# A 64-point second stage on paired column tiles, an inverse on paired row tiles, and PSUM banks given out singly or in pairs, in a kernel of infini-attention and a long convolution

## The chip, the cores and the metric

One core of one Trainium2 chip. The time is the device time of one execution in microseconds (us), from the first to the last instruction of the core. The kernel before takes 365.05 us (median of 3 runs, 364.62 to 369.96).

A run is called slow when it is over 1.5% above the fastest of the same kernel. Below, "ratio" is the mean time of one kernel's fast runs over that of the other's fast runs of the same rounds, so it is not quite the ratio of the medians that I quote. A bracket behind it is its 95% interval. Medians are over all runs, slow ones too.

## The reference, cut to what matters

Two independent parts share the kernel, and their results are laid side by side.

```python
def _A_ref(x, wq, wk, wv, wo, beta):      # 2048 x 576, 32 heads of 18, 4 segments of 512
    q, k, v = ...                         # x @ wq, x @ wk, x @ wv, split into heads and segments
    for s in range(4):
        p = softmax(qs @ ks.T * scale + mask)
        a_dot = p @ vs                    # attention in the segment
        a_mem = (phi(qs) @ M) / (phi(qs) @ z + 1e-6)   # memory of earlier segments
        outs.append(g * a_mem + (1 - g) * a_dot)
        M, z = M + phi(ks).T @ vs, z + sum(phi(ks))
    return o @ wo

def _B_ref(q, k, v, shift_k, ssm_k, ssm_D):   # 2048 x 576
    kv = (causal filter of 4 taps over k) * v
    y = irfft(rfft(kv, 4096) * rfft(ssm_k, 4096))[:2048]   # a long convolution per channel
    return q * (y + kv * ssm_D)
```

## The kernel before

A list scheduler inside the program decides, while the kernel is built, in which order each engine gets its operations. It works with estimated durations and with two long tables of offsets (`SHIFT`, `BIAS`) that were tuned for this kernel. What reaches the chip is a fixed order per engine, and in the traces of this case an engine, or a queue that issues DMAs, that waits for one operation doesn't go on to the next (VectorE below stands 14.4 us although a later operation could run). This will matter.

The Fourier transform is done by matmuls in two stages of the forward transform (`f1`, `f2`) and an inverse. The second stage works on the whole array, with two accumulated matmuls for each result:

```python
def f2(self, A_h, A, k1):
    ...
    for o, tabs in ((0, (self.CS, self.SN)), (1, (self.NSN, self.CS))):
        for n, tab in enumerate(tabs):
            nc.tensor.matmul(pp[:, x, GB * o:GB * o + GB], lhsT=tab[:, k1, :], rhs=src[:, 16 * n + k1, :],
                             start=(n == 0), stop=(n == 1))
    ...   # one PSUM bank and one copy of 384 columns for each of kernel spectrum and input spectrum
```

The 576 columns of x are four tiles of 128 and a remainder of 64. The first 512 rows of x are transposed on TensorE. For the three later segments a transposing DMA brings x in transposed. For the remainder it takes the last 128 columns (448 to 575), of which 64 were in tile 3 already, and the weights of those 64 are zero, so that every matmul of the projections uses the whole array:

```python
def first_x(self, ident):
    x = Tl(self.pl.big, [P, 4, D], BF16, "x0")     # a slot of the ring that holds the sine tables too
    ...
def load_x(self, s):
    for t in range(5):
        c0 = 128 * t if t < 4 else 448
        self.dma(128, lambda dq, t=t, c0=c0: dq.dma_start_transpose(
            out=xT[:, t, :], in_=self.A_x[0, L * s:L * s + L, c0:c0 + P]), w=[(xT, t)], transpose=True)
def proj_qk(self, s, m):
    ...  [nc.tensor.matmul(pq[:], lhsT=self.wqk[:, t, 128 * m:128 * m + P], rhs=xT[:, t, :],
                           start=(t == 0), stop=(t == 4)) for t in range(5)]
```

The softmax here doesn't subtract the row's maximum and nothing guards it: scores larger than these inputs give would overflow.

Of the kernel before, what the change touches and what calls it, by code (L numbers as in the profile page):

```python
# [39 lines left out]
class Slots:  # L40


    def __init__(self, pool, tag, bufs, fifo=True):
        self.pool, self.tag, self.fifo = pool, tag, fifo
        self.slots = [None] * bufs
        self.made, self.given = 0, 0


class Tl:
    def __init__(self, ring, shape, dtype, name):  # L50
        self.ring, self.shape, self.dtype, self.name = ring, shape, dtype, name
        self.left, self.end, self.tile = 0, 0.0, None
        self.no = ring.made
        ring.made += 1
# [4 lines left out]
    def slot(self):  # L59

        r = self.ring
        if r.fifo and r.given != self.no:
            return None
        best = None
        for i, o in enumerate(r.slots):
            if o is None:
                return i, 0.0
            if o.left == 0 and (best is None or o.end < best[1]):
                best = i, o.end
        return best  # L70

    def give(self, i):
        r = self.ring
        r.given += 1
        r.slots[i] = self
        self.tile = r.pool.tile(self.shape, self.dtype, tag="%s%d" % (r.tag, i), name=self.name)
# [6 lines left out]
class Graph:  # L83
# [33 lines left out]
    def run(self):  # L117
# [5 lines left out]
        while left:  # L123
            best = {}
            for o in cand:
                t0, sl = 0.0, []
                for t in o.tiles:
                    if t.tile is None:
                        s = t.slot()
# [14 lines left out]
            for eng, lst in best.items():  # L144
                m = min(x[0] for x in lst)
                lst = [x for x in lst if x[0] <= m + 0.3]
                x = min(lst, key=lambda x: (x[1].prio, x[0]))
                if pick is None or x[0] + x[2] * 0.0 < pick[0][0]:
                    pick = x, eng
            (st, o, us, emit, sl), eng = pick  # L150
            if len(o.alts) > 1:

                h = self.bias.get(o.label, self.bias.get(None, 0.0))
                c = [(x[0] + x[2] + (h if e == ACTQ else 0.0), x, e) for e, l in best.items() for x in l if x[1] is o]
                _, (st, o, us, emit, sl), eng = min(c, key=lambda z: z[0])
# [20 lines left out]
NK1 = 16  # L176
QS = GB // 4
CT0 = [0, 128, 256, 384, 448]
F1D, HXD, NPS, NPJ = 1, 0, 2, 4
# [14 lines left out]
class Pools:  # L194
    def __init__(self, ctx, tc):
# [5 lines left out]
        self.pss = Slots(self.ps, "s", NPS, fifo=False)  # L201
        self.psj = Slots(self.ps, "j", NPJ, fifo=False)
        ring = lambda tag, n: Slots(self.sb, tag, n)
        self.x = ring("x", 1)
        self.stage = ring("st", 5)
# [11 lines left out]
        self.ct = ring("ct", 2)  # L217
        self.HX = ring("H", 3)
        self.Y = ring("Y", 3)
# [3 lines left out]
class Part:  # L223
# [3 lines left out]
    def psj(self, shape, name, dtype=F32):  # L227
        return Tl(self.pl.psj, shape, dtype, name)
# [28 lines left out]
class PartA(Part):  # L257
    def __init__(self, tc, pl, G, ident, A_x, A_wq, A_wk, A_wv, A_wo, A_beta, out):
# [23 lines left out]
        zero(("wz", 0), self.wqk[0:64, 4, :], 2 * D)  # L282
        zero(("wz", 1), self.wv[0:64, 4, :], D)
# [10 lines left out]
        def load_w(dst, w, c0, c1, key, also=()):  # L294
# [3 lines left out]
                dq.dma_start(out=dst[64:128, 4, :], in_=w[512:576, c0:c1])), w=[key], n=2, also=also)  # L298
# [70 lines left out]
    def first_x(self, ident):  # L369

        nc = self.nc
        x = Tl(self.pl.big, [P, 4, D], BF16, "x0")
        self.dma(576, lambda dq: dq.dma_start(out=x[:], in_=self.A_x[0, 0:L, :].rearrange("(t p) c -> p t c", p=P)), w=[x])
        xT = self.xs[0] = Tl(self.pl.x, [P, 5, L], BF16, "xT")
        self.G.label = "tr0"
        for t0, n in ((0, 2), (2, 2), (4, 1)):
            pt = self.psj([P, 2, 4, P], "pt", BF16)

            def tr(t0=t0, n=n, pt=pt):
                for t in range(t0, t0 + n):  # L380
                    c0 = 128 * t if t < 4 else 448
                    for k in range(4):
                        nc.tensor.transpose(out=pt[:, t - t0, k, :], in_=x[:, k, c0:c0 + P], identity=ident[:])
# [5 lines left out]
    def load_x(self, s):  # L389
# [3 lines left out]
        for t in range(5):  # L393
            c0 = 128 * t if t < 4 else 448
            self.dma(128, lambda dq, t=t, c0=c0: dq.dma_start_transpose(
                out=xT[:, t, :], in_=self.A_x[0, L * s:L * s + L, c0:c0 + P]), w=[(xT, t)], transpose=True)


    def store_rows(self, s, kind, tile, r0, f0, n, key):

        qd = self.qk_dram[s]
        self.dma(n, lambda dq: dq.dma_start(out=qd[D * kind + f0:D * kind + f0 + n, :], in_=tile[r0:r0 + n, :]),
# [770 lines left out]
```

## Time and profile before

| | before |
|---|---|
| median of 3 runs | 365.05 us |
| span of the profiled run, mean granted clock | 360.9 us, 0.923 |
| TensorE busy | 296.2 us, 82% |
| VectorE busy | 274.0 us, 76% |
| ScalarE busy | 233.9 us, 65% |
| GpSimd busy | 227.2 us, 63% |

Read it like this: no engine is full over the whole span, yet TensorE is nearly full between 30 and 317 us (the prediction shows the stretches), so a change has to shorten TensorE's work, or fill the ends, to gain. The first is the page's account of the DMA queues (second line: packets, MB, share of 16 engines over the span):

```profile
DMA packets 99860, 56.61 MB, mean 157 GB/s; under 512 B 72286, under 2 KB 92702, under 8 KB 99806
q1 hardware_dynamic: 95518, 54.65, 58.4%
```

```profile
L395 SPq DMA_TRANSPOSE xT<-in_A_x_dram x15: 1142/1259/2603, 49.7 to 176.8; - x15
```

Fifteen loads (5 tiles in 3 segments), all of the kind DMA_TRANSPOSE. The queue SPq, on which SyncE issues them, is held for 1.3 us by each.

### The profile page before, as it was taken

What the parts mean: (1) busy time and instruction counts of PE and PEld (TensorE: products, weight loads), DVE (VectorE), ACT (ScalarE), POOL (GpSimd) and SP (SyncE); (2) the same over time, 40 slices, a digit from 0 to 9 for tenths busy, and PEclk for the clock granted to TensorE, in tenths of its full rate; (3) what the DMA queues carried; (4) which work ended last, traced back from release to release, by engine and by line L of the source; (5) the groups of instructions that cost most, each with busy time, mean ns of one, the idle gap of its engine ahead of it and who ended that gap; (6) DMA issues with size and microseconds to landing.
All of it is one profiled execution on the core that took longest, in us unless ns stands there. A gap on an engine that the chain in (4) does not pass through costs nothing.

```text
span 360.9 us, 7982 instructions
## 1 busy us (share of the span) xinstructions
PE 296.2 (82%) x3048; PEld 171.8 (48%) x3072; DVE 274.0 (76%) x486; ACT 233.9 (65%) x296; POOL 227.2 (63%) x294
## 2 busy tenths in 40 slices
PE   0239998979988987999999697899998979975494
PEld 0136453554444553456644343365565635564283
DVE  7538763866899984778977868559799779789574
ACT  0626048778977877687978846678998767842030
POOL 3500013317999999574396845539799987999800
PEclk9999998999999999899999978599999965999569
DMA  8589656996677419363897764494362543216415
GB/s 241 141 161 172 192 138 146 229 235 201 117 152 205 121 37 202 122 200 96 156 236 202 190 188 161 154 281 171 88 174 59 167 140 123 102 36 202 147 45 144
DMA packets 99860, 56.61 MB, mean 157 GB/s; under 512 B 72286, under 2 KB 92702, under 8 KB 99806
## 3 DMA queue, kind: packets, MB, share of 16 engines
q1 hardware_dynamic: 95518, 54.65, 58.4%
q10 hardware_dynamic: 4304, 1.45, 1.6%
q8 instruction: 24, 0.39, 0.5%
q14 instruction: 14, 0.11, 0.1%
HBM read 25.96 MB, written 21.80 MB: 132 GB/s over the span
## 4 chain that ended last, share of the span: by engine, by line
PE 47%; DMA 17%; DVE 17%; issue 5%; SPq 3%; POOL 3%; ACTq 3%; ACT 3%; DVEq 0%; POOLq 0%
PE sc L518 9%; DMA rt<-a_r_scratch 7%; PE pq L411 6%; PE pout L667 5%; PE pp L910 5%; PE po L568 5%; DMA a_r_scratch<-cs 4%; PE pc L869 4%; PE pf L895 3%; PE pv L450 3%; PE pi L934 3%; ACTq L297 2%; DVE HX L245 2%; POOL Y L947 2%; DMA Dt<-in_B_ssm_D_dram 2%
## 5 line engine op out<-in xcount | busy, mean ns | idle before, releaser
L521 ACT ACTIVATE PT<-sc 128x1024 bf16<-128x1024 f32 x160 | 157.9, 1029 | 33.0 <-PE sc L518 21.5
L526 POOL TENSOR_SCALAR_AFFINE_SELECT PT<-PT 128x512 bf16<-128x512 bf16 (+1 forms) x112 | 80.8, 738 | 68.3 <-ACT PT L521 67.1
L947 POOL TENSOR_TENSOR Y<-HX 128x768 bf16<-128x768 bf16 x48 | 81.9, 1712 | 14.2 <-PE pi L934 9.4
L518 PE MATMUL sc<-qk 18*128 18x512 bf16 (+3 forms) x512 | 60.6, 316 | 5.8 <-ACT PT L521 5.2
L411 PE MATMUL pq<-xT,wqk 128*128 128x512 bf16 x162 | 43.7, 386 | 4.5 <-DVE V L245 2.1
L245 DVE CAST HX<-pp 128x384 bf16<-128x384 f32 x75 | 38.9, 548 | 7.0 <-PE pp L910 6.3
L518 PEld LDWEIGHTS <-qk 18*128 18x128 bf16 x512 | 16.7, 93 | 42.1 <-issue 41.0
L934 PE MATMUL pi<-Y,CST 128*128 128x192 bf16 x96 | 25.0, 266 | 11.2 <-POOL Y L953 8.2
L954 POOL TENSOR_TENSOR Y<-Y 128x192 bf16<-128x192 bf16 x48 | 29.6, 617 | 0.0
L953 POOL TENSOR_TENSOR Y<-Y 128x192 bf16<-128x192 bf16 x48 | 28.4, 592 | 1.4
L245 DVE CAST q<-pq 128x512 bf16<-128x512 f32 x27 | 18.5, 687 | 13.7 <-PE pq L411 12.7
L895 PE MATMUL pf<-W1bd,xs 128*128 128x256 bf16 x144 | 21.8, 288 | 8.0 <-DVE xs L993 7.2
L910 PE MATMUL pp<-A_h,CS 128*128 128x192 bf16 x96 | 24.3, 258 | 3.2 <-DVE A_kv L245 1.4
L411 PEld LDWEIGHTS <-wqk 128*128 128x128 bf16 x180 | 16.5, 99 | 21.9 <-issue 7.7
L450 PE MATMUL pv<-wv,xT 128*128 128x288 bf16 x160 | 26.8, 316 | 0.0
L568 PE MATMUL po<-PT,V 128*32 128x256 bf16 (+3 forms) x512 | 26.0, 328 | 0.4 <-DVE kv L872 0.2
L910 PE MATMUL pp<-A_kv,CS 128*128 128x192 bf16 x96 | 23.6, 253 | 2.7 <-DVE V L245 1.4
L667 PE MATMUL pout<-wo_sb,od 126*128 126x288 bf16 (+1 forms) x160 | 23.6, 291 | 0.2 <-issue 0.2
L910 PEld LDWEIGHTS <-CS 128*128 128x128 bf16 x192 | 18.9, 101 | 9.8 <-issue 9.0
L655 DVE TENSOR_TENSOR nt<-nt,rt 126x1024 bf16<-126x1024 bf16 (+1 forms) x15 | 13.6, 904 | 10.3 <-DMA rt<-a_r_scratch 10.3
L245 DVE CAST A_kv<-pi 128x384 bf16<-128x384 f32 x33 | 17.9, 550 | 3.8 <-PE pi L934 3.3
L450 PEld LDWEIGHTS <-xT 128*128 128x128 bf16 x160 | 16.3, 106 | 9.1 <-issue 2.9
(141 smaller groups left out, 550.6 us busy)
## 6 DMA issues: line engine op xcount, KB each, us to landing
a_o_scratch<-ou SPq DMA_DIRECT2D x12, 512.0 KB
qk<-a_qk_scratch SPq DMA_DIRECT2D x48, 108.0 KB
a_qk_scratch<-q SPq DMA_DIRECT2D x32, 128.0 KB
nt<-a_o_scratch SPq DMA_DIRECT2D x12, 252.0 KB
rt<-a_r_scratch SPq DMA_DIRECT2D x12, 252.0 KB
xs<-kv_scratch SPq DMA_DIRECT2D x3, 768.0 KB
q_sb<-in_B_q_dram SPq DMA_DIRECT2D x3, 768.0 KB
out_dram<-oA SPq DMA_DIRECT2D x16, 144.0 KB
```

Source lines behind the costliest of these rows:

```text
L245: return self.G.op([(DVEQ, dve_us(n, 0.53 if bf else 1.042), lambda: nc.vector.tensor_copy(out=out(), in_=in_())), (ACTQ, act_us(n), lambd ...
L411: nc.tensor.matmul(pq[:], lhsT=self.wqk[:, t, 128 * m:128 * m + P], rhs=xT[:, t, :], start=(t == 0), stop=(t == 4)) for t in range(5)],
L450: nc.tensor.matmul(pv[:], lhsT=xT[:, t, P * tt:P * tt + P], rhs=self.wv[:, t, 288 * h:288 * h + 288], start=(t == 0), stop=(t == 4)) for t ...
L518: nc.tensor.matmul(ps[:, b, off:off + n], lhsT=qk[r, 2 + u, P * kt:P * kt + P], rhs=qk[r, u, P * kt:L], start=True, stop=True, tile_positi ...
L521: self.act(act_us(1024), lambda: nc.scalar.activation(out=dst(), in_=ps[:], func=ACT.Exp, scale=self.scale), r=[ps], w=[key])
L526: self.pool(0.2 + n * 0.13, lambda: nc.gpsimd.affine_select(out=ap(), in_=ap(), compare_op=ALU.is_ge, fill=0.0, base=0, pattern=[[0, n], [ ...
L568: nc.tensor.matmul(po[32 * j:32 * j + 32, P * kt:L], lhsT=V[:, kt, 19 * h:19 * h + 32], rhs=rhs, start=(kt == 0), stop=(kt == 3), tile_pos ...
L667: nc.tensor.matmul(ps[:], lhsT=o[0:K, t, P * qt:P * qt + P], rhs=self.wo[0:K, t, 288 * h:288 * h + 288], start=(t == 0), stop=(t == 4)) fo ...
L895: self.pe(pe_us(*[256] * w), lambda cc=cc, ps=ps: [nc.tensor.matmul(ps[:, u, :], lhsT=xs[:, cc + u, :], rhs=self.W1[:].rearrange("p e k -> ...
L910: nc.tensor.matmul(pp[:, x, GB * o:GB * o + GB], lhsT=tab[:, k1, :], rhs=src[:, 16 * n + k1, :], start=(n == 0), stop=(n == 1))
L934: nc.tensor.matmul(pp[:, o, :], lhsT=tab[:, k1, :], rhs=Y[:, n, :], start=(n == 0), stop=(n == 1))
L947: nc.gpsimd.tensor_tensor(out=Y[:].rearrange("p (x h) c -> p x h c", x=2), in0=HX[:, 1, :].rearrange("p (x c) -> p x c", x=2).unsqueeze(2) ...
```

## The change

Its intent: let the second stage use 64 frequencies at a time on two column tiles side by side, which halves its matmul time. Let the inverse contract 64 rows on two row tiles. Copy two PSUM banks at once. Load x first. Let VectorE take some of the spectral products from GpSimd. Along with it, and to save the zero weights, the 64 remaining columns of x are handled as 64: loaded twice, into the lower and the upper half of the partitions, and multiplied in one half of the array. The core of the diff (cut; the tuning tables are replaced as well):

```diff
-        self.pss = Slots(self.ps, "s", NPS, fifo=False)
-        self.psj = Slots(self.ps, "j", NPJ, fifo=False)
+        self.banks = Slots(self.ps, "b", 8, fifo=False)          # given out singly or in even pairs
 ...
+    pl.x0 = Tl(pl.big, [P, 4, D + 64], BF16, "x0")               # before the sine tables
 ...
     def load_x(self, s):
-        for t in range(5):
-            c0 = 128 * t if t < 4 else 448
-            self.dma(128, lambda dq, t=t, c0=c0: dq.dma_start_transpose(
-                out=xT[:, t, :], in_=self.A_x[0, L * s:L * s + L, c0:c0 + P]), w=[(xT, t)], transpose=True)
+        for t, h in ((0, 0), (1, 0), (2, 0), (3, 0), (4, 0), (4, 1)):
+            q, n = (slice(0, P), P) if t < 4 else (slice(64 * h, 64 * h + 64), 64)
+            self.dma(n, lambda dq, t=t, q=q, n=n: dq.dma_start_transpose(
+                out=xT[q, t, :], in_=self.A_x[0, L * s:L * s + L, P * t:P * t + n]), w=[(xT, t + h)], transpose=True)
 ...  # the last tile of a Q/K projection; the value projection likewise
+            r = slice(64 * i, 64 * i + 64)
+            nc.tensor.matmul(out, lhsT=self.wqk[r, 4, 128 * m:128 * m + P], rhs=xT[r, 4, :], start=False, stop=True,
+                             tile_position=(64 * i, 0))
 ...  # second stage
+                    for b in range(2):
+                        nc.tensor.matmul(pp[64 * b:64 * b + 64, x, GB * o:GB * o + GB], lhsT=tab[:, 2 * r + b, :],
+                                         rhs=src[:, 2 * r + b, :], start=True, stop=True, tile_position=(0, 64 * b))
 ...  # inverse
+                            nc.tensor.matmul(ap(b)[:, o, :], lhsT=tab[q, r + 8 * h, :], rhs=Ys[h][q, n, :],
+                                             start=(h == n == 0), stop=(h == n == 1), tile_position=(64 * b, 0))
 ...  # products: GpSimd or VectorE, as the scheduler sees fit
+        self.G.op([(POOLQ, 1.72, lambda: mul(nc.gpsimd)), (DVEQ, 1.0, lambda: mul(nc.vector))], [HX], [Y])
```

## The prediction

> **What bounds the kernel now.** I read the page first (shares of the span), then the busy time of each engine in five stretches, then the timeline of the start, then TensorE's timeline in the middle. The stretches carry the argument. Their columns are: stretch in us, its length, then busy us (and instructions) of each engine, granted clock, DMA share, GB/s.
>
> ```profile
> core 0: us, PE busy (x) PEld busy (x) DVE busy (x) ACT busy (x) POOL busy (x), PEclk, DMA share, GB/s
> 0.00:30.00 30.00, 8.29 (x71) 7.06 (x72) 16.73 (x37) 9.95 (x10) 7.75 (x23) 1.00 0.78 188
> 30.00:90.00 60.00, 55.38 (x506) 29.01 (x511) 41.43 (x102) 36.97 (x52) 15.60 (x24) 0.97 0.81 184
> 90.00:200.00 110.00, 99.60 (x1109) 56.01 (x1118) 92.72 (x153) 89.50 (x113) 88.11 (x109) 0.98 0.64 156
> 200.00:317.00 117.00, 106.05 (x1094) 58.99 (x1100) 91.14 (x148) 87.49 (x109) 91.15 (x112) 0.87 0.51 151
> 317.00:361.00 44.00, 26.88 (x277) 20.68 (x274) 32.00 (x50) 10.02 (x17) 24.59 (x30) 0.79 0.37 116
> ```
>
> From 30 to 317 us TensorE is busy 55.4 + 99.6 + 106.1 = 261 of 287 us (91%); no other engine exceeds 85% in any of these stretches. So the middle is set by TensorE, with VectorE, ScalarE and GpSimd not far below. The first 30 us hold 8.3 us of TensorE work and the last 44 us 26.9: there something else decides. For the start, the timeline names it:
>
> ```profile
> 0.81 0.46 SPq L297 DMA_DIRECT2D wqk<-in_A_wq_dram  x1
> ...
> 12.69 1.57 DVE L799 TENSOR_SCALAR gw<-fpat,pcol_f 128x2048 int32<-128x2048 int32 x1 [4.46 <-ACT W1bd L762]
> 16.16 0.52 SPq L298 DMA_DIRECT2D wv<-in_A_wv_dram  x1
> ...
> 18.39 0.52 SPq L373 DMA_DIRECT2D x<-in_A_x_dram  x1
> ...
> 28.61 1.28 PE L383 MATMUL pt<-ident,x 128*128 128x128 bf16 x20
> ...
> 30.60 4.48 PE L411 MATMUL pq<-xT,wqk 128*128 128x512 bf16 x19
> ```
>
> The first tile of x shares a three-slot ring with the sine tables and is made after four of them, so its load cannot be issued before the angle pattern is read for the last time (12.7 to 14.3 us), and then stands in line on the queue behind wv (16.2), until 18.4 us; it is transposed at 28.6, and the first projection runs at 30.6. Yet the query weights were requested at 0.8 us. TensorE lacks work for want of x. Meanwhile it spends 1.9 + 1.9 us on transposing tables (groups CST and SNT).
>
> For the middle, these five consecutive lines of TensorE show what the modes of its array cost (start, busy, what):
>
> ```profile
> 240.98 0.79 PE L667 MATMUL pout<-wo_sb,od 126*128 126x288 bf16 x5
> 241.71 0.39 PE L518 MATMUL sc<-qk 18*128 18x384 bf16 x4
> 242.03 0.26 PE L934 MATMUL pi<-Y,CST 128*128 128x192 bf16 x1
> ...
> 242.37 1.24 PE L411 MATMUL pq<-xT,wqk 128*128 128x512 bf16 x4
> 243.45 0.25 PE L910 MATMUL pp<-A_h,CS 128*128 128x192 bf16 x1
> ```
>
> I use start to start, since the ends are modelled. Four pi matmuls of 192 columns take 242.37 - 242.03 = 0.34 us, 80 ns each plus almost nothing, when whole-array work follows. Five pout of 288 columns take 0.73 against 5 x 0.12 = 0.60 when a score burst (18 rows, two row tiles side by side) follows; the score burst takes 0.32 for 384 + 128 = 512 columns (0.213). So each passage between whole array and tiles costs about 0.11 us, and row tiles do run side by side (four matmuls of 1024 columns in all took the time of 512). Column tiles do so too: the 16 attention-value matmuls in four column tiles start at 238.74 and the next burst at 239.40, 0.66 us, against 0.53 if four overlap and 2.1 if none does.
>
> **What the Trainium skill says.** "TensorEngine Tiling (Array Packing)", section Tiling Modes, Key Properties: different tiles load weights and multiply in parallel, but changing the mode drains the engine. The trace agrees on both: 0.66 us for sixteen, and the 0.11 us per passage above. The same page, section Performance Considerations, PSUM Bottleneck: tiling does not shorten the evacuation of PSUM, which may become the limit; here VectorE at 84% in 90 to 200 us is near it. The same page, section Restrictions, says that column tiling turns fast weight load off; no row of this profile isolates that. "DMA: Bandwidth & Descriptors", section Why small descriptors are slow: about 3 cycles are added to each packet, 256 bytes being 8 beats. The channel-tile load xs goes from 256-byte to 128-byte runs, so by that page 7 cycles twice instead of 11, an estimate of 1.27 times; the chain of waits has one such load at 4.80 us, so some 1.3 us more in each of six, off TensorE's path unless it comes up short of work.
>
> **The change, part by part.** Times are start to start at full clock.
>
> Second stage of the forward transform: before, 384 matmuls of 192 columns, 384 x 0.083 = 31.9 us. After, 384 of half width, two side by side, 192 x 0.083 = 15.9. Minus 16.0 us.
>
> First stage: before 144 x 0.109 (256 columns) = 15.7. After 36 chunks of 8 pairs of 128 columns. If weights hide, 8 x 0.056 = 0.45 us each, 16 in all; if each pair is held up by its weights like the table transposes and back transposes (16 in 1.23 us, 0.077 each), 0.62 and 22 in all. I take +3.5 us.
>
> Inverse: 192 whole-array matmuls become 384 in two row tiles, 192 pairs: the same 16 us. Value projection: 10 matmuls become 9 slots, 16 x 0.12 = minus 1.9.
>
> Mode passages: the Q/K projection now ends each of 36 accumulations with a 64-row tile, the value projection each of 16, and first stage, second stage and inverse are tiled where they used to sit side by side with whole-array bursts. Fewer bursts (the second stage has 48 instead of 96, inverse 24 instead of 48) take some back. I count 50 inside the projections and about 30 around the transform: 80 x 0.11 = +9 us. TensorE in the middle: -16.0 + 3.5 - 1.9 + 9 = about -5 us.
>
> PSUM copies, from the rows of the costliest groups: a VectorE copy takes 548 ns for 384 elements, 687 for 512 and 1220 for 1024, so about 1.05 ns an element and 0.15 fixed; ScalarE 482 for 384 and 1020 for 1024. HX: 96 copies, about 51 us, become 48 of 768 at 0.95 or 0.80, about 44. Inverse 25 to 22, V 14 to 11.5, output projection 14 to 12, attention values 37 to 33, the feature map about 4 less. In sum some 23 us off VectorE and ScalarE together (274 + 234). GpSimd keeps its products (48 x (1.71 + 0.62 + 0.59) = 140 us) and masks (81 us), but products may now go to VectorE. With less copying and one common pool of banks I expect TensorE's 26 idle us of the middle to shrink by 4.
>
> Start: x goes first. Its 0.66 MB and the 0.74 MB of query weights, at the 224 GB/s measured in the first 10 us, need about 6 us; with issue and latency I put the first projection at 10 us instead of 30.6. From 10 to 30 us TensorE can do about 17 us of useful work instead of 4.5 (8.3 less the 3.8 of table transposes): 12.5 us moved forward, at 91% fill about -13 us. Added tables (two more sines of 1.9 us, two patterns of 1.9 us on GpSimd, about 5 us on VectorE) fall where those engines idle.
>
> Tail: the last attention unit goes through reciprocals, two DMA steps and the output projection (last exp at 318, last weights stored at 330, last product with them at 348). None of that is removed; GpSimd's products of the last group, which last to 342, can be shared. I give it -2 us.
>
> Sum: 365 - 13 - 5 - 4 - 2 = 341 us.
>
> **Rivals.** (a) Mode passages eat the transform's gain. For: 0.11 us each is measured, and nearly every burst now differs from its neighbour. With 150 of them and the slow first stage TensorE's middle rises by about 5 us: 351. (b) The early start does not carry through: the first score waits for stored and reloaded heads (stored 36.1, first score 49.7), the exponentials must follow all sines, and the kv chain may set when the convolution starts. Against it: between 30.6 and 49.7 TensorE was full, so those waits were hidden behind work. If half is lost: 348. (c) Paired banks: eight banks are four pairs, where there were two pairs and four singles; a 1.2 us copy holds two banks. If TensorE waits more for banks, the gain of 4 turns into a loss of 8: 353. (d) Everything goes well, weights hide and few passages are added: 328.
>
> **Range and chances.** The start is the surest part (8 to 17 us); the middle could be anything between -20 and +5. Two of the rivals together give about 355, all three about 360. So 341 with 328 to 355. Faster by over 2% means below 357.7: it takes the early start alone plus a neutral rest, 0.86. Within 2%: 0.11. Slower: 0.03.
>
> **What would show each step.** First Q/K projection near 10 us, and 15 us or more of TensorE busy by 30 us; if it comes after 20, the start is wrong. Eight second-stage matmuls start to start in 0.33 to 0.45 us: if 0.65, column tiles do not overlap. First-stage chunks in 0.45 to 0.62. HX copies: 48 of 768 elements, 0.95 us on VectorE. A Q/K projection of five at 1.2 to 1.3 us instead of 1.08 shows the passages. Idle of TensorE attributed to copies, above 26 us in the middle, shows rival (c). If the first score comes as late as 45 us, rival (b) holds.

## The result, and the profile after

The changed kernel is correct and takes **625.11 us** (median of 4 runs, 621.92 to 628.70, all fast). The kernel before took 366.68 us in the same job (364.62 to 369.96). The ratio is 1.7036 [1.6862, 1.7210]. The prediction said 341 and gave slower by over 2% a chance of 0.03.

The page of the changed kernel, busy time first, then the DMA lines that answer to those of before:

```profile
PE 308.8 (50%) x3664; PEld 163.7 (26%) x3664; DVE 281.3 (45%) x400; ACT 243.0 (39%) x272; POOL 186.0 (30%) x249
DMA packets 314210, 56.95 MB, mean 92 GB/s; under 512 B 286442, under 2 KB 307050, under 8 KB 314154
q1 hardware_dynamic: 306650, 54.94, 112.1%
```

The engines work about as long as before (TensorE 309 instead of 296 us, VectorE 281 instead of 274, ScalarE 243 instead of 234, GpSimd 186 instead of 227), but the span is 620 us, so they stand still. The bytes are nearly the same, 56.95 instead of 56.61 MB. The packets are three times as many, and the packets of queue q1 overlap so much that they take 112% of the engines' span. The waits name the place (waiting engine, tile and line, releaser; us in total, times, longest):

```profile
PE banks L451 <- DMA xT<-in_A_x_dram: 230.8, 6, 42.9
ACT q L275 <- PE banks L451: 172.1, 8, 82.5
```

Six waits for one load, 231 us in sum. Line 451 is the last matmul of a projection. The view of the tile xT (engine, operation and count, then minimum, median and maximum ns) says which load it is:

```profile
L424 SPq DMA_TRANSPOSE xT<-in_A_x_dram x12: 1122/1248/2474, 54.6 to 350.9; - x12
L424 SPq DMA_DIRECT2D xT<-in_A_x_dram x6: 651/687/42422, 60.9 to 352.9; - x6
```

All eighteen were written as transposing loads in one line of the program. Twelve, 128 columns wide, are of the kind DMA_TRANSPOSE. The six of 64 columns have become plain copies, DMA_DIRECT2D. And SyncE's queue shows what such a copy does to those behind it (start, length, what):

```profile
60.93 0.69 SPq L424 DMA_DIRECT2D xT<-in_A_x_dram  x1
61.72 38.05 SPq L431 DMA_DIRECT2D a_qk_scratch<-q  x2
99.82 0.65 SPq L424 DMA_DIRECT2D xT<-in_A_x_dram  x1
100.56 39.16 SPq L958 DMA_DIRECT2D kv_scratch<-kv  x1
```

The copy itself is issued in 0.69 us, and the next issue then holds the queue for 38 us. So I read a long issue here as the mark of the transfer before it. The stretches of the prediction, in the changed kernel (columns as there):

```profile
0.00:30.00 30.00, 4.39 (x25) 2.57 (x25) 12.04 (x39) 4.08 (x4) 9.91 (x25) 1.00 0.77 162
30.00:90.00 60.00, 36.80 (x301) 15.73 (x302) 32.91 (x62) 30.32 (x33) 10.54 (x15) 0.84 1.22 75
200.00:317.00 117.00, 32.10 (x453) 16.21 (x445) 30.73 (x34) 26.71 (x31) 25.23 (x31) 0.61 1.54 44
```

From 200 to 317 us TensorE works 32 of 117 us, while the DMA engines count 1.54 times full for 44 GB/s. The first 30 us hold 4.4 us of TensorE's work, fewer than the 8.3 of before, and not the 15 that were predicted. That is a second error, hidden behind the first. TensorE at the start:

```profile
9.82 1.89 PE L412 MATMUL banks<-ident,x 128*128 128x128 bf16 x16 [9.82 <-DMA x<-in_A_x_dram]
13.83 0.61 PE L412 MATMUL banks<-ident,x 128*128 128x128 bf16 x4 [2.12 <-DMA x<-in_A_x_dram]
28.11 1.87 PE L447 MATMUL banks<-xT,wqk 128*128 128x512 bf16 x4 [13.67 <-DVE xT L274]
```

x does come early and is transposed at 10 to 14 us, but the first projection starts at 28.1 us, after 13.7 us of waiting for VectorE's copy of xT. Before, it was at 30.6. ScalarE's queue and VectorE show why:

```profile
2.85 0.65 ACTq L966 DMA_DIRECT2D xs<-in_B_ssm_k_dram  x1
7.79 5.01 ACTq L929 DMA_DIRECT2D sk_bf<-in_B_shift_k_dram  x1
17.67 0.35 ACTq L930 DMA_DIRECT2D sk_bf<-in_B_shift_k_dram  x1
19.34 0.42 ACT L836 ACTIVATE W1bd<-k1pat 128x256 bf16<-128x256 int32 x1
```

```profile
19.86 1.35 DVE L874 TENSOR_SCALAR gw<-fpat,pm_f,o_re 128x2048 int32<-128x2048 int32 x1 [14.43 <-ACT W1bd L836]
26.84 1.22 DVE L274 COPY xT<-banks 128x2048 bf16<-128x2048 bf16 x1
```

ScalarE issues the 768 KB load of xs, then two small loads, and stands in the issue of those until 18 us. Only then does it make its first sine. VectorE needs that sine's buffer for an operation that comes before the copy of xT in its order, and so stands for 14.4 us, though x has been in PSUM since 14. The trace of the kernel before could have warned of this. There too ScalarE stood in an issue behind the load of xs, for 7.5 us, and made its first sine only after it:

```profile
1.97 0.82 ACTq L885 DMA_DIRECT2D xs<-in_B_ssm_k_dram  x1
2.82 7.52 ACTq L297 DMA_DIRECT2D wqk<-in_A_wk_dram  x1
```

### The profile page after: what moved, and what is told of

It reads as the page before. It is cut to its first block, busy times and chain, and to the rows that moved or that the text cites. A ratio compares the mean times of both kernels' runs of the same rounds, so it can differ in the third digit from the quotient of the medians.

```text
span 619.7 us, 9092 instructions
## 1 busy us (share of the span) xinstructions
PE 308.8 (50%) x3664; PEld 163.7 (26%) x3664; DVE 281.3 (45%) x400; ACT 243.0 (39%) x272; POOL 186.0 (30%) x249
## 2 busy tenths in 40 slices
DMA packets 314210, 56.95 MB, mean 92 GB/s; under 512 B 286442, under 2 KB 307050, under 8 KB 314154
## 4 chain that ended last, share of the span: by engine, by line
DMA 37%; PE 21%; another core or an unknown queue 13%; DVE 10%; SPq 10%; issue 4%; ACT 3%; POOL 1%; ACTq 0%; DVEq 0%; POOLq 0%
DMA xT<-in_A_x_dram 22%; SPq L958 6%; PE banks L447 5%; DMA xs<-in_B_ssm_k_dram 4%; DMA rt<-a_r_scratch 3%; DMA qk<-a_qk_scratch 2%; PE banks L725 2%; ACT PT L584 2%; PE banks L579 2%; PE banks L628 2%; SPq L424 2%; DMA q_sb<-in_B_q_dram 2%; PE banks L451 2%; PE banks L981 2%
## 5 line engine op out<-in xcount | busy, mean ns | idle before, releaser
L584 ACT ACTIVATE PT<-banks 128x1024 bf16<-128x1024 f32 x160 | 155.8, 1030 | 51.9 <-PE banks L579 47.2
L451 PE MATMUL banks<-xT,wqk 64*128 64x512 bf16 x36 | 16.8, 468 | 230.8 <-DMA xT<-in_A_x_dram 230.8
L274 DVE CAST q<-banks 128x512 bf16<-128x512 f32 x23 | 15.6, 687 | 125.0 <-PE banks L451 84.2
L1036 POOL TENSOR_TENSOR Y<-HX 128x768 bf16<-128x768 bf16 x25 | 43.4, 1740 | 93.4 <-ACT e L474 82.2
L274 DVE CAST A_kv<-banks 128x768 bf16<-128x768 f32 (+1 forms) x26 | 27.6, 1077 | 89.5 <-PE banks L1018 87.3
L579 PE MATMUL banks<-qk 18*128 18x384 bf16 (+3 forms) x512 | 54.3, 329 | 21.2 <-DMA qk<-a_qk_scratch 10.6
L447 PE MATMUL banks<-xT,wqk 128*128 128x512 bf16 x144 | 47.4, 462 | 19.1 <-DVE xT L274 13.7
L1042 POOL TENSOR_TENSOR Y<-Y 128x192 bf16<-128x192 bf16 x32 | 21.3, 665 | 94.9 <-DVE Y L1036 94.0
L274 DVE CAST ou<-banks 128x1024 bf16<-128x1024 f32 (+1 forms) x27 | 29.7, 1101 | 8.9 <-PE banks L631 8.4
L628 PE MATMUL banks<-PT,V 128*32 128x256 bf16 (+3 forms) x512 | 30.0, 365 | 1.8 <-ACT PT L584 0.9
L274 DVE CAST HX<-banks 128x768 bf16<-128x768 f32 x26 | 24.6, 951 | 8.6 <-PE banks L999 8.4
L500 PEld LDWEIGHTS <-xT 128*128 128x128 bf16 (+1 forms) x160 | 13.8, 102 | 50.4 <-issue 46.6
L981 PE MATMUL banks<-W1bd,xs 128*64 128x128 bf16 x576 | 24.5, 245 | 2.6 <-ACT PT L584 2.3
```

Source lines behind the costliest of these rows:

```text
L274: return self.G.op([(DVEQ, dve_us(n, 0.53 if bf else 1.042), lambda: nc.vector.tensor_copy(out=out(), in_=in_())), (ACTQ, act_us(n), lambd ...
L447: nc.tensor.matmul(out, lhsT=self.wqk[:, t, 128 * m:128 * m + P], rhs=xT[:, t, :], start=(t == 0), stop=False)
L451: nc.tensor.matmul(out, lhsT=self.wqk[r, 4, 128 * m:128 * m + P], rhs=xT[r, 4, :], start=False, stop=True, tile_position=(64 * i, 0))
L500: nc.tensor.matmul(out, lhsT=xT[r, t, P * tt:P * tt + P], rhs=self.wv[r, t, 288 * h:288 * h + 288], start=(t == 0), stop=(t == 4), **({} i ...
L579: nc.tensor.matmul(ps[:, j - j0, off:off + n], lhsT=qk[r, 2 + u, P * kt:P * kt + P], rhs=qk[r, u, P * kt:L], start=True, stop=True, tile_p ...
L584: self.act(act_us(512 * w), lambda out=out, ps=ps: nc.scalar.activation(out=out(), in_=ps[:], func=ACT.Exp, scale=self.scale), r=[ps], w=[ ...
```

## The experiments

All were correct unless said otherwise.

**First: is it the narrow load?** e1 replaces the two 64-column loads by one 128-wide transposing load and a small copy inside the core's memory. e2 puts the two narrow loads, and nothing else of the change, into the kernel before. e3 is e1 without the copy: the upper 64 rows are used in all projections.

```diff
 e1  -  dma_start_transpose(out=xT[q, 4, :], in_=x[..., 512:576])          # twice, for each half
     +  dma_start_transpose(out=xT[:, 4, :], in_=x[..., 448:576])
     +  dma_start(out=xT[0:64, 4, :], in_=xT[64:P, 4, :])
 e2  (before)
     -  dma_start_transpose(out=xT[:, 4, :], in_=x[..., 448:576])
     +  [dma_start_transpose(out=xT[64*h:64*h+64, 4, :], in_=x[..., 448+64*h:512+64*h]) for h in range(2)]
```

> The changed kernel with one edit: the last tile of x is loaded by one transposing load of 128 columns, as before the change, and its upper half is then copied to the lower half by a small plain DMA, so that the 64-row pairs stay. Theory A (the two 64-column loads are no longer done as transposes but element by element, some 35,000 packets each, and all the loss comes from them): packets fall from 314,000 to about 115,000, the 231 us of TensorE waiting for xT go, and the time is 330 to 365 us. Rival B (the mode passages of TensorE, the common pool of banks or the schedule cost most): still above 450 us.

> The kernel before with one edit: the last tile of x in each of the three later segments comes by two transposing loads of 64 columns instead of one of 128. Nothing else of the change. Theory A: packets rise by about 210,000 to 310,000, TensorE waits about 200 us or more for xT, and the time is 560 to 640 us. Rival B: within 10% of the kernel before.

> As e1, but without the copy: every last 64-row product uses the upper half of the tile, so the value projection loses its row pairs (16 slots of 288 columns more, about 2 us of TensorE) and one DMA per segment goes. Theory A: 330 to 365 us, within 1.5% of e1. Rival B: above 450 us. If e3 is faster than e1, the copy's landing time is on the path.

e1: 391.33 us (388.06 to 391.86), ratio 1.0739 [1.0647, 1.0832]. e2: **605.39 us** (603.34 to 610.33), ratio 1.6665 [1.6543, 1.6787]. e3: 387.28 us (386.47 to 392.80), ratio 1.0641 [1.0585, 1.0697]; its profiled run was slow. The kernel before stood at 364.55 us in that job. In e2 the same six copies and the same flood of packets appear:

```profile
L396 SPq DMA_DIRECT2D xT<-in_A_x_dram x6: 692/19460/39912, 55.1 to 335.7; - x6
DMA packets 294933, 56.61 MB, mean 94 GB/s; under 512 B 267359, under 2 KB 287775, under 8 KB 294879
```

So these six loads alone make the old kernel nearly as slow as the changed one (+241 us), and taking them out of the changed one takes 234 us away. It is settled, with one part undone and with that part done alone. What remains is that the change without them is still 6 to 7% slower than before, where I had expected 7% faster. The narrow loads are not why.

**Second: what of the rest, with the scheduler free.** e4 is e3 with the two small loads of the shift filters on SyncE's queue. e5 is e3 with the last 64 rows multiplied in the whole array, with zero weights, as before. e6 and e7 empty the tuning tables of the kernel before and of e3.

```diff
 e4  -  ... n=2, also=[ACTQ])        +  ... n=2, also=[])
 e5  -  matmul(out, lhsT=wqk[r, 4, ...], rhs=xT[r, 4, :], tile_position=(64 * i, 0))
     +  matmul(out, lhsT=wqk[:, 4, ...], rhs=xT[:, 4, :])
 e6, e7  -  SHIFT = {...}   BIAS = {...}     +  SHIFT = {}   BIAS = {None: 0.3}
```

> e3 with one edit: the two tiny loads of the shift filter go out on SyncE's queue instead of ScalarE's. In e1 ScalarE stands behind them until 17.2 us (the issue of the second waits while the 768 KB channel tile with 128-byte runs drains from the same queue), so the first sine table comes at 18.9 us and, in VectorE's order, the copy of x behind it at 26.5; the first projection is at 27.6. Theory C (this blocked issue is what kept the early x from helping): first projection at 13 to 18 us and 6 to 12 us off the time of e3, some 376 to 381 us. Rival (what follows the start is bound elsewhere): first projection early, but the time within 3 us of e3.

> e3 with the last tile of the Q, K and V projections back in the whole array (zeros in the lower half of the weights, 128-row products), so that none of the 52 accumulations ends in a 64-row tile. The rest is e3. Theory D (mode passages cost about 0.11 us each): the 36 last products fall from about 0.35 to 0.22 us start to start, TensorE's sum falls by 5 to 8 us, and the time by as much where it is the bound: 379 to 384 us. Rival (TensorE is no longer the bound in e3, it is idle 75 us): less than 2 us.

> The kernel before with its two tables of hand-tuned order (the shifts and the engine choices) emptied, so that the list scheduler orders by plain rank. It shows what the tuning is worth. I expect 375 to 400 us. If it is within 2% of the kernel before, the order matters little and the loss of e3 is not one of order.

> e3 with its two tables of order emptied in the same way. Theory S (e3 loses 23 us because its order was tuned for loads that land early and does not fit the chip; its structure is no worse): within 10 us of e6, on either side. Rival T (the structure is worse: paired banks, mode passages, products on VectorE): 20 us or more above e6.

e4: 394.41 us (385.39 to 397.05), only one run fast, so no ratio; its first projection came at 22.3 us, not at the 13 to 18 expected. e5: 412.29 us (409.86 to 417.85), 1.1209 [1.1107, 1.1312]. e6: 383.69 us (380.82 to 385.77), 1.0449 [1.0346, 1.0552]. e7: 402.68 us (398.73 to 407.38), 1.0866 [1.0763, 1.0970]. The kernel before: 367.05 us.

e5 takes work and mode passages away and is 25 us slower than e3. Any such edit makes the scheduler choose a new order on all engines. That the new order costs the 25 us is inferred here; e10 below makes the same edit with the order held and loses nothing. So these four measure the order more than the edit, and e1 and e3 carry the same flaw in their last few per cent. e6 against e7 is the cleaner pair, neither of them tuned: the changed structure is slower there too, by 19 us in medians and 15 in fast runs (398.9 against 383.5), so a lucky table for the kernel before isn't the whole reason. From here on I change only what an operation emits and leave the scheduler's list alone, and compare every engine's order instruction by instruction.

**Third: the changed kernel in exactly its own order.** e8 differs from the changed kernel only in the last-tile load (128 wide, then the copy, in the places of the two narrow ones). e9 is e8 with the shift filters' loads issued on SyncE. e10 is e8 with the last tile in the whole array and no copy. e11 is e8 with all spectral products on GpSimd.

```diff
 e9   -  ACTq: xs, sk_bf, sk_bf                 +  ACTq: xs        SPq: wq, x, sk_bf, sk_bf, wk, ...
 e10  as e5, in the order of e8
 e11  -  (DVEQ, 1.0, lambda: mul(nc.vector))    +  (DVEQ, 1.0, lambda: mul(nc.gpsimd))   # same place in the order
```

> The changed kernel with every engine's instructions in exactly its own tuned order (compared instruction by instruction: nothing differs but SyncE's loads of the last tile of x): one transposing load of 128 columns, then a plain copy of its upper half to the lower. e1 and e3 had let the list scheduler reorder; e5 showed that a reordering alone can cost 25 us. Theory S (order): clearly below e1 and e3, 345 to 370 us. Rival T (structure): 380 to 395 us, as e1 and e3.

> e8 with the two tiny shift-filter loads on SyncE's queue instead of ScalarE's, all else in the same order. Theory C (the blocked issue on ScalarE kept the early x from helping): first projection at 13 to 20 us instead of 27, and 5 to 12 us off e8. Rival: first projection early, time within 3 us of e8.

> e8 with the last tile of the projections in the whole array (128 rows, zeros below), all else in the same order; the copy of half a tile is not needed and falls away. Theory D (mode passages): last products of a projection 0.22 to 0.25 instead of 0.35 us start to start, 4 to 8 us off e8. Rival: within 3 us.

> e8 with all spectral products and sums on GpSimd, as in the kernel before, in the same program order. Theory E (VectorE loses by the 20 or so products it took over, and holds up the PSUM copies): GpSimd busy back to some 225 us, VectorE down by 30 to 40, time 5 to 10 us below e8. Rival (sharing helps, GpSimd would be in the way): 5 us or more above e8.

e8: 386.50 us (379.51 to 389.81), three of four runs slow, no ratio. Its one fast run is 1.028 of the mean of the fast runs before (369.06). e9: 383.29 us (379.05 to 392.30), 1.0343 [1.0225, 1.0461]. e10: 378.05 us (376.37 to 385.93), 1.0216 [1.0107, 1.0326]. e11: 396.73 us (393.89 to 400.42), 1.0720 [1.0623, 1.0816]. The kernel before: 369.44 us.

Four readings follow. With its own order kept, the loss is 3% (e8's one fast run) to 5% (medians, mostly of slow runs) instead of 6 to 7, so part of e1's excess was probably its new order. e11 says that VectorE's help with the products is not the culprit: without it the time is 10 us more by medians, and 16 by fast runs (395.8 against e8's only one, 379.5). The rows of e10 against those of e8 show what a passage between the array's modes costs. Here are three consecutive rows of TensorE in e8 (four matmuls on the whole array, one on half of it, the next projection), then in e10:

```profile
35.22 1.04 PE L455 MATMUL banks<-xT,wqk 128*128 128x512 bf16 x4
36.19 0.39 PE L459 MATMUL banks<-xT,wqk 64*128 64x512 bf16 x1
36.51 1.04 PE L455 MATMUL banks<-xT,wqk 128*128 128x512 bf16 x4
```

```profile
28.59 1.03 PE L456 MATMUL banks<-xT,wqk 128*128 128x512 bf16 x4
29.46 0.38 PE L459 MATMUL banks<-xT,wqk 128*128 128x512 bf16 x1
29.67 1.03 PE L456 MATMUL banks<-xT,wqk 128*128 128x512 bf16 x4
```

Start to start 36.51 - 35.22 = 1.29 us against 29.67 - 28.59 = 1.08, at full clock in both: 0.21 us for two passages, the 0.11 each of the prediction. What that is worth in the whole, these two runs can't tell: 8 us by medians, 2 us by fast runs (379.5 against the mean 377.5). Nor do they differ in the passages alone: e10 also drops the three copies of the half tile and the small weight loads that the second half needs, and its first projection comes at 24.9 us, not 28.5. e9 has its first projection at 18.5 instead of 28.5 us, as wished, but is no faster: VectorE then stands until 32.2 us in front of the next thing in its order, an addition that needs a small load (Dt) that SyncE issues only at 19.8 us:

```profile
32.23 0.37 DVE L1091 TENSOR_TENSOR xs<-xs,Dt 128x48 bf16<-128x48 bf16 x1 [13.79 <-issue]
```

The profile names no releaser for this wait ("issue"). That it was Dt is inferred; in e8 the same addition waits for Dt by name, and in e12, where Dt comes early too, it runs at 16.8 us.

**Fourth: is the early start worth anything once it gets through?** e12 is e10 with the shift filters' loads and the Dt load issued on SyncE right behind x. e13 is the kernel before with the early x alone, which the scheduler reorders.

```diff
 e12  -  ACTq: xs, sk_bf, sk_bf     SPq: wq, x, wk, wv, wo, beta, Dt, ...
      +  ACTq: xs                   SPq: wq, x, sk_bf, sk_bf, Dt, wk, wv, wo, beta, ...
 e13  -  x = Tl(self.pl.big, [P, 4, D], BF16, "x0")        # in first_x, after the tables
      +  pl.x0 = Tl(pl.big, [P, 4, D], BF16, "x0")         # before the tables
```

> The version of e10 (the changed kernel in its own order, 128-wide transposing load for the last tile of x, last K tile in the whole array), with two more moves and nothing else: the two small loads of the shift filters and the small load of Dt are issued on SyncE right behind x's load (before: the shift filters on ScalarE behind the 768 KB load of xs, Dt on SyncE behind the weights). Theory W (the early start of the first projection is real, but it is eaten by VectorE, which stands in order before the addition of Dt): first projection at about 18 us instead of 24.9 in e10, and, unlike e9, the first value projections come as much earlier as well (about 38 us instead of 44.9); time down by 5 to 9 us from e10's 378, to 369 to 373, that is 1.00 to 1.015 of before. Rival N (what happens before 45 us is hidden behind the later stages, where other waits set the pace): the burst of value projections comes earlier, but the time stays at 375 to 380. Rival Q (the loads compete with x and the weights): first projection not before 22 us, time as e10 or worse.

> The kernel before with one part of the change alone: the tile for the first rows of x takes the first place in the ring of large buffers, as in the change, so that its load needn't wait for the tables. The scheduler reorders the rest by itself, so a few per cent either way can be the order (e5, e6). If an early x is worth what the prediction said (13 us, first projection at about 10 us instead of 30.6): 350 to 355 us. If the sines and the Dt load in VectorE's order hold it back as they do in the changed kernel: first projection at 20 to 28 us, and 355 to 372 us. If the new order costs as it did in e5: 375 to 390 us.

e12: 371.03 us (363.34 to 373.47), 1.0071 [0.9938, 1.0204], four of six runs slow. e13: 393.48 us (389.38 to 397.22), 1.0799 [1.0714, 1.0883]. The kernel before: 366.20 us. In e12 the start is now what the change intended:

```profile
9.27 2.32 PE L413 MATMUL banks<-ident,x 128*128 128x128 bf16 x20 [9.27 <-DMA x<-in_A_x_dram]
15.58 1.86 PE L456 MATMUL banks<-xT,wqk 128*128 128x512 bf16 x4 [3.99 <-DVE xT L274]
```

The first projection is at 15.6 us instead of e10's 24.9, the first value projection at 30.4 instead of 44.9, and the time is 7 us below e10's by medians and 5 by ratios (1.0071 against 1.0216), in another job and with intervals that overlap. So the start is probably worth something, though these runs do not separate it from nothing. What is shown is that waits in order for small loads kept it from TensorE in the changed kernel. e13 has x even earlier (first projection at 11.3 us) and is 8% slower than before. Its stretches, then those of the kernel before:

```profile
0.00:150.00 150.00, 116.86 (x1061) 55.32 (x1073) 88.48 (x192) 99.06 (x123) 41.60 (x76) 0.87 0.71 171
300.00:394.00 94.00, 65.17 (x652) 41.80 (x650) 60.65 (x101) 40.90 (x51) 61.24 (x74) 0.78 0.34 111
```

```profile
0.00:150.00 150.00, 114.72 (x1184) 64.76 (x1199) 108.85 (x217) 94.44 (x122) 78.35 (x109) 0.98 0.72 167
300.00:361.00 61.00, 43.88 (x454) 30.69 (x452) 45.42 (x72) 23.33 (x33) 39.95 (x46) 0.81 0.35 113
```

TensorE did as much in the first 150 us as before, but GpSimd 42 us instead of 78, and it has 61 us of work left after 300 us: the new order put attention first and the spectral products last. As a test of the early x this run is spoilt by its order. A version of the kernel before with x early and all else in place did not fit into the core's memory (131 KB per partition asked for, 127 KB left, an error of the build and no run), so what an early x is worth there stays open.

**Fifth: where the rest went.** TensorE's largest waits in e12 are for loads and for VectorE. e14 moves two blocks in VectorE's order (about twenty small operations for the gates, which stood before the convolution's products; and the division of the softmax sums, behind one more product). e15 moves two loads in SyncE's order besides. e16 moves one more pair: two transposing loads of phiK go behind the small load of the sums (cs).

```diff
 e14  VectorE:  -  gates, kv, kv, ..., dg    +  kv, kv, ..., dg, gates
                -  cs, kv                    +  kv, cs
 e15  SyncE:    -  q_sb (768 KB), 8 transfers, ...     +  8 transfers, q_sb, ...
                -  kv (k, transposing), qk x4          +  qk x4, kv
 e16  SyncE:    -  phiK x2, qk, e, cs        +  qk, e, cs, phiK x2
```

> e12 with two blocks moved in VectorE's order and nothing else: the gate columns (some twenty small operations, 48.5 to 54.1 us in e12) go behind the first two convolution tiles, and the division of the sums (3 operations, which stood 6.6 us in front of a load) goes behind the next product kv. Theory V (the time that TensorE no longer works has become waits for VectorE's in-order queue, here 2.9 us at 55 us and 5.8 us at 204 us): those two waits of TensorE fall below 1 us each, and the time falls by 3 to 8 us from e12's 371. Rival F (TensorE only waits for the next late thing, a load from SyncE's queue): the two waits go, others take their place, time within 2 us of e12.

> e14, and two loads moved in SyncE's order: the 768 KB load of q_sb (not needed before 158 us) behind the next eight transfers, and the transposing load of k for the last channel tile behind the four qk loads, one of which TensorE awaited for 6.0 us at 230 us in e12. Theory V with the queues of SyncE: the wait for the qk load at 230 us falls from 6.0 to below 1 us, the wait for the kv load at 92 us from 4.0 to below 2 us; 3 to 8 us less than e14, 355 to 366 us, so faster than before by up to 2%. Rival F: no more than 2 us less than e14.

> e15 with one more move in SyncE's order: the two transposing loads of phiK (4.9 us of SyncE's queue from 192.4 us) go behind the small load of the sums (cs), for which VectorE stood 6.7 us before 203.9 us and TensorE behind it 5.2 us. phiK is read at 208.9 us only. Theory V: VectorE's wait for cs falls from 6.7 to about 2 us, TensorE's wait behind it from 5.2 to under 1 us, time 3 to 5 us below e15: 362 to 365 us, 0.986 to 0.993 of before. Rival F: the wait goes on to phiK or to a later load, time within 2 us of e15.

e14: 372.15 us (369.08 to 374.64), 1.0132 [1.0075, 1.0189]. e15: 367.49 us (364.91 to 370.59), 0.9998 [0.9953, 1.0043]. Both beside 367.29 us of the kernel before. e16: 365.28 us (362.60 to 369.78), 0.9981 [0.9917, 1.0045], beside 366.93 us.

e14 was a miss: the two waits that I named went, and a third came in their place. VectorE stands before the division of the sums in either order, and the product behind it was simply no longer the one that TensorE missed first. In e15:

```profile
203.89 0.35 DVE L699 TENSOR_SCALAR cs<-cs,ea 128x256 f32<-128x256 bf16 x1 [6.74 <-DMA cs<-a_o_scratch]
```

e15's moves in SyncE's order gained 5 us against e14 in the same job. e16 shortened the wait of the line above from 6.7 to 3.7 us, not to 2 as expected, and TensorE's wait behind it from 5.3 to 4.1. Against e15, of another job, it gained 2 us by medians and 0.6 by ratios, which the intervals don't separate from nothing.

**Sixth: the mode passages once more.** e17 is e16 with the last tile in half of the array again, as the change has it, and so with the three copies of the half tile and the small weight loads that go with it. e18 is e16 repeated beside it.

> e16 with one thing put back as the change has it: the last 64 rows of the Q/K and value projections in half of the array (36 + 32 matmuls with a tile position, so about 70 more passages of TensorE between its modes), and with it the copy of the last tile of x to the lower partitions. Same order on every engine. Theory M (a passage costs about 0.11 us on TensorE's path): 4 to 8 us slower than e18, which is e16 once more in the same job: 369 to 374 us. Rival F (TensorE waits for others anyway, so the passages vanish in its idle time; the difference of e8 and e10 was mostly the slow state, fast runs 379.5 against 377.5): within 2.5 us of e18.

> e16 unchanged, so that e17 is compared with it in one job: 363 to 367 us in its fast runs, 0.99 to 1.005 of before.

e17: 369.30 us (361.70 to 374.18), five of six runs slow, no ratio. e18: 364.93 us (359.07 to 369.52), 0.9934 [0.9843, 1.0025]. The kernel before: 366.45 us. By medians e17 is 4.4 us slower. The only fast run of e17 (361.7) is within e18's fast ones (359.1 to 364.2). So the passages, with the copies and loads that go with them, cost between nothing and some 5 us, and I leave it there. In e17 the first projection also came 2.9 us later than in e18 (18.3 against 15.4). The best version that came of this, e16 and e18, is not to be told from the kernel before: both intervals hold 1, and together they reach from 0.984 to 1.005.

The stretches of e18, in answer to those of the prediction:

```profile
0.00:30.00 30.00, 16.71 (x142) 8.92 (x144) 25.89 (x49) 11.41 (x13) 13.35 (x28) 1.00 0.70 139
30.00:90.00 60.00, 47.33 (x417) 22.27 (x413) 34.24 (x70) 39.04 (x43) 12.89 (x21) 0.85 0.87 179
90.00:200.00 110.00, 100.68 (x1481) 57.46 (x1478) 95.63 (x122) 88.36 (x101) 75.76 (x93) 0.96 0.75 166
200.00:317.00 117.00, 98.31 (x1295) 52.25 (x1296) 96.06 (x119) 90.46 (x102) 74.20 (x95) 0.85 0.59 158
```

The start is 8.4 us fuller than before (16.7 against 8.3). The stretch from 30 to 90 us is 8.1 us emptier (47.3 against 55.4). So the gain of the start is handed back at once. TensorE's waits between 30 and 90 us add up to 13 us in e18, against 4 before. The largest three are these:

```profile
PE banks L522 <- DVE q L290: 3.3, 1, 3.3
PE banks L472 <- ACT ou L291: 3.1, 1, 3.1
PE banks L601 <- DMA qk<-a_qk_scratch: 2.2, 1, 2.2
```

Two are copies out of PSUM, one is the reload of stored heads, and DMA (0.87 of its capacity in this stretch, 0.81 before) is about as full as before. The first copy, of q, itself stood behind the store of an earlier q: it waits 4.2 us for that store (4.0 in e12), which holds a staging buffer, and of these the change has three of double size, each held until both its halves are stored, instead of five.

## Why the prediction was wrong, point by point

**The term that was missing: the last tile of x.** This is the step that failed. The prediction counted the two 64-row tiles as TensorE's work (mode passages) and didn't price their load at all; none of its four rivals touches it. It was in the diff, as one line in a loop that looked like the old one, with 64 for 128. It cost 241 us where it was done alone (e2) and 234 to 239 us where it was undone (e1; e8, 386.5 against 625.1, of another job). The size follows from the page: (314,210 - 119,379 packets in e8) / 6 = 32,472 packets for each load, and 64 x 512 = 32,768 is the number of its two-byte elements. So I read the load as going element by element. TensorE waited six times, 38.5 us on average, which are the 231 us of the wait. The Trainium skill had it: "DMA: Bandwidth & Descriptors", section DMA Transpose (X-bar), Constraints, says that for an input in DRAM of less than 128 in the free dimension the software can fall back to a rearranged access pattern, with inefficient descriptors. The trace agrees, with DMA_DIRECT2D in place of DMA_TRANSPOSE. I had cited that page for its packet overhead (1.27 times for xs) and stopped reading there.

**"Start: first projection at 10 us instead of 30.6", "about -13 us", "the surest part".** Wrong in the changed kernel. x was there at 9.8 us, the projection came at 28.1. The step that failed is the silent assumption that VectorE is free to copy what TensorE has transposed. It stood in its fixed order behind sines, which stood behind ScalarE's issue of loads, which stood behind the 768 KB load of xs. Taken out of the way (e9 for ScalarE, e12 for the Dt load as well), the projection came at 15.6 us and the time fell by 5 to 7 us, within the noise. So if the mechanism exists, it has at most about half the size of the term, at the price of two moves that the change does not have. (The term's own division gives 12.5 / 0.91 = 13.7, not 13. And the 128-byte runs of xs, estimated at 1.27 times, come to 1.44 by the median packet in the trace's records, 2 x 13 ns in e10 against 18 ns before; that moved the end of this load little: its last packet starts at 15.3 us in e10, 16.6 in the changed kernel, 15.7 before.) Rival (b), that the early start doesn't carry through, held by the prediction's own sign: the first score came at 46.6 us in the changed kernel (49.6 before, 36.8 in e12). It named the wait for reloaded heads and the kv chain. Both are there: between 30 and 317 us TensorE waits 10.2 us for reloaded heads (qk) and 11.0 for VectorE's kv products in e10, and 8.5 and 1.9 in e18, against 0 and 1.3 before. It did not name the loads of a few KB.

**"TensorE in the middle: about -5 us."** Right in its parts. I worked out the time that TensorE is occupied by adding the distances from start to start of its matmuls, without the waits of over 0.15 us, at whatever clock was granted. Second stage 40.0 us before, 24.3 in e18 (predicted -16.0 at full clock, measured -15.7). First stage 18.5 and 20.8 (predicted +3.5, measured +2.3). Inverse 24.0 and 22.2 (predicted the same). The second stage of one tile HX, at full clock in e8:

```profile
108.23 0.27 PE L1007 MATMUL banks<-A_h,FR 128*64 128x192 bf16 x2
108.33 0.25 PE L1007 MATMUL banks<-A_h,FI 128*64 128x192 bf16 x2
108.42 0.25 PE L1007 MATMUL banks<-A_kv,FR 128*64 128x192 bf16 x2
108.50 0.25 PE L1007 MATMUL banks<-A_kv,FI 128*64 128x192 bf16 x2
108.68 0.39 PE L587 MATMUL banks<-qk 18*128 18x256 bf16 x4
```

Eight in 0.45 us with a passage at the end, inside the 0.33 to 0.45 that was to show it: column tiles overlap. The passages cost 0.11 each, as said. Over the whole, TensorE is occupied 298 us before and 291 in e18. e18 has neither the passages in the projections nor the shorter value projection, so the sum that answers to it is -16.0 + 3.5 + 30 x 0.11 = about -9; it measured -7, at a mean clock of 0.890 against 0.923. The sum was about right. That it would shorten the kernel was not.

**"With less copying ... I expect TensorE's 26 idle us of the middle to shrink by 4."** The copies came as counted (HX: 26 of 951 ns on VectorE and 22 of about 800 on ScalarE). But the idle time grew. Between its first and last matmul TensorE idles 44 us before, 75 in e10, 52 in e18. Account for e18 against before: TensorE starts 5.5 us earlier (9.0 instead of 14.5), works 6.7 us less, idles 8.1 us more, and the stretch after its last matmul is 0.4 us longer; the sum, -3.7, is the difference of the two profiled spans (357.2 and 360.9). So the gain of the transform is there, and became waits. The waits put down to PSUM copies between 30 and 317 us are 15.4 us before, 14.6 in e10 and 19.4 in e18: they did not shrink by 4, and they stay under the 26 that was to show rival (c). What is new in e10 are the waits for reloaded heads and kv products above. That the other engines' in-order queues deliver at their old pace is my explanation and not shown by itself. VectorE is as busy as before (280 us against 274), because it took products from GpSimd in place of the copies that it lost; e11 speaks for taking them.

**The tail (-2 us)** was not tested by itself.

**What stays open.** How much of the remaining difference is clock: e12 to e18 are granted 0.87 to 0.90 in their fast runs, the kernel before 0.91 to 0.93. The Trainium skill, "TensorE: Matmul & The Clock Gate", Part 1, says that the clock is set by how busy TensorE has been, half rate after idleness. The rows of the traces agree in kind: in e12, after 4 us of idleness, the first projection takes 2.09 us from start to start (15.58 to 17.67), a later one 1.08. The granted clock of the profile reads 1.00 all through these rows, so it doesn't record this slowness. So more waits can cost clock as well, but no run here separates the two. What the mode passages cost in the end (0 to 5 us, together with the copies that go with them). What an early x would bring to the kernel before. Whether pairing of PSUM banks helps or harms, which no run isolated.

## What to carry to other kernels

Price every line of a diff that has a DMA in it, first of all where a width changes, and look in the changed kernel's trace for the *kind* of each transfer: a transposing load that turned into a plain copy gives itself away by packet count long before anyone looks at time. Before counting an earlier arrival as a gain, follow it through the fixed order of each engine up to the matmul that needs it; the small loads on the way decide. And when a kernel's order is made by a tuned scheduler, an edit measures the new order too (25 us in e5, as far as can be inferred), so hold the order still and compare it engine by engine.

## What the Trainium skill lacked or had wrong

- "DMA: Bandwidth & Descriptors", section DMA Transpose (X-bar), Constraints, names the fallback for narrow inputs without its packets or its sign in a trace. The same page, section Rules for kernel authors, puts a plain DMA with a rearranged access pattern at a 19 times difference in general. Here a 512 x 64 load of 64 KB became about 32,500 packets of the kind DMA_DIRECT2D and kept TensorE waiting 38 us on average, at some 2 GB/s; the 128-wide load beside it is a DMA_TRANSPOSE that is issued in 1.3 us.
- The same page, section Issuing engines are not separate DMA queues, says that the time to initiate a DMA is usually small beside the DMA itself. It was not, here, behind a load with many small packets: ScalarE stood in the issue of two loads of a few KB until 18 us (5.0 us in the first alone), and SyncE 38 us in the next issue after a narrow load.
- "TensorEngine Tiling (Array Packing)", section Key Properties, says that a change of mode drains TensorE but gives no time. Here two passages cost 0.21 us (1.29 against 1.08 us for a projection), and 36 + 16 projections with them changed the whole by 0 to 5 us only, the copies that go with them included.
